# A weight ring of four slots instead of five, a 49th resident weight chunk, and two TensorE steps moved by a chunk

## The chip, the cores and the metric

The kernel runs on one core of one Trainium2 chip. The time is device microseconds from start to end of one execution; the figure for a kernel is the median over its runs. One execution was also taken by the hardware profiler; it has its own time, and a span from its first to its last instruction.

## The reference, cut to what matters

Two independent parts are computed and put side by side in the output. Part A is a shift and a long convolution over 2048 positions and 1024 channels. Part B is an attention over 64 segments of 32 tokens with 8 memory tokens that are handed from segment to segment:

```python
for s in range(n_seg):
    h = concatenate([mem, x[:, s*32:(s+1)*32]])          # 40 tokens x 1024
    q, k, v = (einsum('btd,dhe->bhte', h, W) for W in (Wq, Wk, Wv))   # 32 heads of 128
    p = softmax(where(mask, q @ k.T * scale, -1e9))
    o = einsum('bhte,hed->btd', p @ v, Wo)
    mem = o[:, :8]                                        # needed by the next segment
    outs.append(o[:, 8:])
```

Segment s + 1 can't begin before segment s has its memory rows, so part B is a chain of 64 segments. Each of them multiplies by all of Wq, Wk, Wv and Wo, 32 MB in bf16, while the on-chip memory (SBUF) holds less than that.

## The kernel before, in words

**Chunks.** The weights of part B are cut into 64 chunks of 128 x 2048 bf16 (512 KB): `(m, kc, g)` for K (m = 0), Q (1) and V (2), with eight slices kc of the contracted dimension and two halves g of the heads; `(3, hp, 0)` for Wo, two heads each. `ORDER` (L25 to L27) lists them in the order in which a segment uses them, and a chunk is called here by its place in that list, 0 to 63: K half 0 and Q half 0 interleaved (0 to 15), K half 1 (16 to 23), Q half 1 (24 to 31), V half 0 (32 to 39), V half 1 (40 to 47), Wo (48 to 63).

**Resident and streamed.** `STREAM` (L28) names the chunks that don't stay in SBUF: 16, of which two (56 and 57, `KEPT_A` and `KEPT_B`) are copied into spare room in PSUM and one small tile during segment 0. The other 14 are loaded anew in each segment from a copy in DRAM, `WS`. The other 48 chunks are resident, in tiles that the trace calls Wmid, Wres, Wmore, Wlate, pw and Wring.

**The ring.** Streamed chunks go through the slots of a ring: tiles `wring0`, `wring1`, `wring3` to `wring5`, in the order of the list `free` (L705). `fetch()` (L712) takes the next load of the list, takes the first free slot and issues the load on SP's queue (L716). `done(ch)` (L853) is called after a chunk's last matmul in the segment; it puts the slot back in the list and fetches. SP takes its instructions in the order written, so a load that waits for its slot holds back all behind it. Ahead of segment 0 two loads are issued (L745), and `RING - 2` more at the start of the loop (L886).

**Tiles with two lives.** `wring0` and `wring1` hold a transposed input (XBT) until the V matmuls ahead of the segments are through; `wring2` and `wring3` are the staging tiles (`pair`, L485) from which V of the new tokens is stored to DRAM (VBD<-pair). `wring2` then becomes the home of one resident chunk (L770), chunk 6, the first K chunk of the order's second group.

**Late loads.** `late` (L443, reordered in L747) lists resident chunks whose homes come free only near the end of part A; `place_late` (L722) takes the next of them and issues its load, also on SP. `at_hand` names V chunks that still lie in another chunk's home during segment 0; there `done` issues that home's load.

**A segment** (L1033 to L1107) is written out by hand inside `tc.manual_schedule()`, so instructions go to each engine in the order of the text; ahead of it a planner sets the order. `Proj.run(n)` (L922) issues n chunks of a projection, four matmuls of 128 x 512 each, and calls `done` after each chunk. `evac` (L934) lets ScalarE cast the result to bf16 (L936). `transposes` (L939, matmuls in L942) turns it on TensorE into the tile `tps`, from which it is copied to KT or QT. `scores` (L945), `softmax_a` (VectorE, then an exponential on ScalarE, L962), `softmax_b` (VectorE), `attend` (L988) and `evac_o` (a ScalarE cast of the attended values to OT, L1004) follow for each half. The output product (`out_half`, L1014) uses a Wo chunk in two passes f, each of four matmuls of 128 x 256; the four chunks of FIRST and the five of LAST do all their f = 0 passes before the first f = 1 pass, so a streamed chunk among them is held longer. POOL issues the loads of a segment's input (rec, L869) and of its part of V (VBs, L907) and the stores of the output (L1106).

Of the kernel before, what the change touches and what calls it, by code (L numbers as in the profile page):

```python
# [9 lines left out]
BF = mybir.dt.bfloat16  # L10
# [14 lines left out]
ORDER = [(0, kc, 0) for kc in (0, 1, 4, 5)] + [(1, kc, 0) for kc in (0, 1)] + [(0, kc, 0) for kc in (2, 3, 6, 7)] + \  # L25
    [(1, kc, 0) for kc in range(2, 8)] + [(m, kc, 1) for m in (0, 1) for kc in range(8)] + \
    [(2, kc, g) for g in range(2) for kc in range(8)] + [(3, hp, 0) for hp in O_ORDER]  # L27
STREAM = (1, 7, 13, 18, 24, 30, 35, 41, 46, 49, 53, 56, 57, 58, 60, 62)  # L28
N2, N3 = 12, 19
WO_COPY = 29  # L30
Q_LOAD = (10, 13, 16, 19)
X_LOAD = 1
RING = 5

PITCH = 2048
SCRATCH = 1024
# [383 lines left out]
def b_kernel(ctx: ExitStack, tc, x, mem0, Wq, Wk, Wv, Wo, outb, n_seg, run_a):  # L420
# [13 lines left out]
    streamed = set()  # L434
    for i in STREAM:
        streamed.add(order[i])
# [6 lines left out]
    late = [ch for ch in resident if ch not in placed]  # L443
# [12 lines left out]
    def stream_src(ch):  # L456
        return WS[ring_order.index(ch), :, 0:2048]
# [18 lines left out]
    base = ctx.enter_context(tc.tile_pool(name="b0_base", bufs=1, side="right", reuse_waits="tile"))  # L476
# [3 lines left out]
    def xbt(kc):  # L480
        return XBT[kc // 4][:, kc % 4]
# [3 lines left out]
    def pair():  # L485
        turns["pair"] ^= 1
        return base.tile([128, 2048], BF, tag=f"wring{2 + turns['pair']}", name="pair")

    def slot16(shape, dt, name):
        turns["stage"] ^= 1  # L490
        return base.tile(shape, dt, tag=f"stage{turns['stage']}", name=name)
# [3 lines left out]
    def pw(k=None):  # L495
        if k is None:
            k = pw_next[0] % 8
            pw_next[0] += 1
        return pring.tile([128, 2048], BF, tag=f"pw{k}", name="pw")
# [63 lines left out]
    def group(m, g, temps={}, which=range(8), ws=None, eng=nc.sync, held=False):  # L563
        ws = ws or [None] * 8
        for kc in which:
            ch = (m, kc, g)
            if ch in res:
                got.append(eng.dma_start(res[ch], dram_chunk(ch)))
                ws[kc] = res[ch]
            else:  # L570
                t = temps[ch]() if ch in temps else pw()
                got.append(eng.dma_start(t[:], dram_chunk(ch)))
                if ch in streamed:
                    copies.append((stream_src(ch), t[:]))
                ws[kc] = t[:]
        while copies and not held:
            copied.append(nc.gpsimd.dma_start(*copies.pop(0)))
        return ws
# [28 lines left out]
    def evac(dst, src):  # L607
        flip[0] += 1
        if flip[0] % 3:
            nc.scalar.copy(dst, src)  # L610
        else:
            nc.vector.tensor_copy(dst, src)
# [35 lines left out]
    def store():  # L648
        if stores:
            nc.scalar.dma_start(*stores.pop(0))  # L650
# [40 lines left out]
    def more(i):  # L691
        return wres3.tile([128, 2048], BF, tag=f"Wmore{i}", name="Wmore")
# [5 lines left out]
    order_s = [ch for ch in order if ch in streamed]  # L698
    kept = {KEPT_A: "A", KEPT_B: "B"}
    at_hand = {}  # L700
# [1 line left out]
             if s == 0 and ch not in v_temp[2:] or s > 0 and ch not in kept]  # L702
    live = {}
    now = [0]
    free = [4, 5, 0, 1, 3]  # L705

    def slot():
        k = free.pop(0)
        t = (base if k < 4 else ring).tile([128, 2048], BF, tag=f"wring{k}", name="wring")
        return k, t  # L710

    def fetch():  # L712
        if loads:
            s, ch = loads.pop(0)
            live[s, ch] = k, t = slot()
            nc.sync.dma_start(t[:], stream_src(ch))  # L716

    def place(ch, ap):
        res[ch] = ap
        nc.sync.dma_start(dst_view(ap, ch), dram_chunk(ch))  # L720

    def place_late(n, tile_of):  # L722
        chs = [late.pop(0) for _ in range(n)]
        t = tile_of()
        for i, ch in enumerate(chs):
            place(ch, t[:, 2048 * i:2048 * i + 2048])
# [4 lines left out]
    with c0p:  # L731
        temps = dict(zip(v_temp, homes_v))
        wv = [group(2, 0, temps), None]
        for _ in rest:
            store()
        wv[1] = group(2, 1, temps)
        for i, ch in enumerate(v_temp):
            if i >= 2:
                home = (lambda i=i: more(i)) if i < len(v_temp) - 2 else (lambda k=i - len(v_temp) + 4: pw(k))
                at_hand[ch] = (wv[ch[2]][ch[1]], home)  # L740
        while stores:
            store()
        with tc.issue_after(got[-1].ins):
            for _ in range(2):
                fetch()  # L745
        n_k = len(own[0, 0])
        late = late[n_k:-1] + late[4:n_k] + late[:4] + late[-1:]  # L747
        for g in range(2):
            ws = wv[g]
            if g == 0:  # L750
                vsts = slot16([128, 4, 4, 512], BF, "vst")
            for tb in range(4):
                vst = vsts[:, tb] if g == 0 else pair()[:].rearrange("p (c w) -> p c w", c=4)
                for c in range(4):
                    ps = ps0.tile([128, 512], F32, tag="ps0", name="vb_ps")
                    for kc in range(8):
                        nc.tensor.matmul(ps[:], lhsT=xbt(kc)[:, 16 * tb:16 * tb + 16, :].rearrange("p s t -> p (s t)"),  # L757
                                         rhs=ws[kc][:, c * 512:(c + 1) * 512], start=(kc == 0), stop=(kc == 7))
                    evac(vst[:, c, :], ps[:])
                nc.scalar.dma_start(  # L760
                    VBD[16 * tb:16 * tb + 16, :, :, :, g * 128:(g + 1) * 128].rearrange("s t c i e -> (s t) (c i) e"),
                    vst.rearrange("p c (i e) -> p (c i) e", i=4))
            if g == 0:
                with tc.issue_after(got[-1].ins):
                    place_late(4, stage_home)
                    for i in [*range(len(v_temp) - 2, n_more), *range(len(v_temp) - 2)]:
                        place_late(1, lambda: more(i))
                    place_late(1, lambda: pw(2))
                    place_late(4, stage_home)
        place_late(1, lambda: base.tile([128, 2048], BF, tag="wring2", name="Wring"))  # L770
        assert len(late) == len(at_hand)

    one = ctx.enter_context(tc.tile_pool(name="b_one", bufs=1, side="right", reuse_waits="tile"))
    two = ctx.enter_context(tc.tile_pool(name="b_two", bufs=2, side="right", reuse_waits="tile"))
# [39 lines left out]
    def keep(ch):  # L814
        t = live[0, ch][1]
        if kept[ch] == "A":
            w = t[:].bitcast(I32).rearrange("p (hh dh f x) -> p hh f dh x", hh=2, dh=2, f=2)
            for q in range(4):
                bits(OTi[:, q, 160:416].rearrange("p (dh x) -> p dh x", dh=2), w[:, q // 2, q % 2])
        else:  # L820
            w = t[:].bitcast(I32)
            for q in range(4):
                for home, at in B_homes[q]:
                    n = home.shape[1] * (home.shape[2] if len(home.shape) == 3 else 1)
                    if len(home.shape) == 3 and n > 128:
                        for dh, o in enumerate(quarter_cols(q)):
                            bits(home[:, 2 * dh:2 * dh + 2, :], w[:, o // 2:o // 2 + 128].rearrange("p (b x) -> p b x", b=2))
                        continue
                    for dh, o in enumerate(quarter_cols(q)):
                        lo, hi = max(at, 128 * dh), min(at + n, 128 * dh + 128)  # L830
                        if lo < hi:
                            src = w[:, o // 2 + lo - 128 * dh:o // 2 + hi - 128 * dh]
                            bits(home if len(home.shape) == 3 else home[:, lo - at:hi - at], like(src, home))
# [19 lines left out]
    def done(ch):  # L853
        if now[0] == 0 and ch in at_hand:
            place_late(1, at_hand[ch][1])
        elif ch in streamed and (now[0] == 0 or ch not in kept):
            if now[0] == 0 and ch in kept:
                keep(ch)
            free.append(live.pop((now[0], ch))[0])
            fetch()  # L860

    P_pad = one.tile([128, 5, 64], BF, name="P_pad")
# [22 lines left out]
    with tc.manual_schedule():  # L885
        for _ in range(RING - 2):  # L886
            fetch()
# [14 lines left out]
        for s in range(n_seg):  # L902
# [133 lines left out]
            q0 = Proj(1, 0)  # L1036
            fill_mem(hT, Y, 1)
            q0.run(2)
            k0 = k0.run(4).evac()
            q0.run(3)  # L1040
            KT0 = keys(0)
            nc.vector.tensor_copy(KT0[:, :, :, 0:32], transposes(k0))  # L1042
            q0 = q0.run(3).evac()
            k1 = Proj(0, 1).run(4)
            QT0 = one.tile([128, 4, 4, 32], BF, tag="QT", name="QT")
            nc.vector.tensor_copy(QT0[:], transposes(q0))
# [11 lines left out]
            V0 = pv0.run(4).evac()  # L1058
            scores(1, QT1, KT1)
            E1 = softmax_a()  # L1060
            pv1 = Proj(2, 1).run(4)
            attend(0, PT0, V0)
            OT0 = evac_o(0)
            PT1 = softmax_b(E1)
            pv1.run(4)
            if not last:
                load_x(s + 1)
            V1 = pv1.evac()
# [110 lines left out]
```

## Time and profile before

| what | us |
|---|---|
| median of 3 runs | 1865.01 (1863.74 to 1870.66) |
| the profiled execution's own time | 1864.63 |
| its span | 1862.8 |
| TensorE busy | 1737.2 |
| VectorE busy | 1009.7 |
| ScalarE busy | 680.8 |
| POOL busy | 267.2 |
| start of segment 1's VBs load, and of segment 63's | 486.0, 1839.0 |
| mean rate of the DMA engines | 340 GB/s |

"Busy" counts the time in which an engine executes, not the time in which its sequencer waits or issues. The page cuts the span in 40 slices of 46.6 us and gives the busy share of each in tenths. In a time line, a row has start and duration in us, engine, line of the kernel, operation, tiles (out<-in) and shapes; the bracket at its end is the idle time of the engine before the row and what ended it. PE is TensorE's matmuls, PEld its weight loads. A queue of DMA issues has a q behind its engine's name (SPq). Matmuls overlap, so their durations add to more than the time they take: the steps between their starts tell more.

### The profile page before, as it was taken

How to read it: one execution, taken by the hardware profiler on the slowest of the kernel's cores; microseconds unless marked ns; L12 is line 12 of the kernel's file. 1: busy time of each engine (PE TensorE's matmuls, PEld its weight loads, DVE VectorE, ACT ScalarE, POOL GpSimd, SP SyncE). 2: the span in 40 equal slices, each digit the busy share in tenths (PEclk: the TensorE clock that was granted, in tenths of full speed). 3: DMA queues.
4: the chain of work that ended last, by engine and by line, in shares of the span. 5: the costliest groups of instructions: out<-in, count | busy, mean ns of one | idle time of the engine just before them, and what ended most of it. 6: DMA issues, size and time to landing. Idle time of an engine off the chain costs nothing.

```text
span 1862.8 us, 68333 instructions
## 1 busy us (share of the span) xinstructions
PE 1737.2 (93%) x29492; PEld 1000.3 (54%) x29492; DVE 1009.7 (54%) x3391; ACT 680.8 (37%) x1195; POOL 267.2 (14%) x501
## 2 busy tenths in 40 slices
PE   6989996767999999999999999999999999999998
PEld 3433322323565666666566655566566656566665
DVE  9927873201555555555555555555555555555555
ACT  6945650111333333333333333333333333333333
POOL 4003341000111111111111111111111111111111
PEclk9999998888999999999999999999999999999999
DMA  9989889996999999999999999999999999999997
GB/s 333 372 301 316 291 270 326 309 307 197 343 353 358 357 352 359 352 352 356 360 357 356 349 338 351 352 368 356 350 355 357 353 349 354 351 363 358 348 360 292
DMA packets 232946, 632.45 MB, mean 340 GB/s; under 512 B 72818, under 2 KB 72834, under 8 KB 232644
## 3 DMA queue, kind: packets, MB, share of 16 engines
q1 hardware_dynamic: 160548, 558.83, 81.4%
q0 software_dynamic: 17344, 46.17, 6.8%
q10 hardware_dynamic: 54752, 23.07, 4.6%
q8 instruction: 231, 3.78, 0.8%
q14 instruction: 71, 0.58, 0.1%
HBM read 572.94 MB, written 58.72 MB: 339 GB/s over the span
## 4 chain that ended last, share of the span: by engine, by line
PE 68%; DMA 20%; ACT 5%; DVE 5%; issue 2%; ACTq 0%; POOL 0%; POOLq 0%; DVEq 0%; SPq 0%
PE acc L927 26%; PE yacc L1014 20%; DMA wring<-WS 15%; PE kb_ps L621 6%; PE tps L942 4%; PE vb_ps L757 3%; DMA REC<-stage 2%; ACT OT L1004 2%; ACT qkv_sb L936 1%; ACT s_sb L246 1%; DVE mx L957 1%; DVE E L959 1%; PE tps L874 1%; PE OTp L992 1%; PE s_ps L244 1%
## 5 line engine op out<-in xcount | busy, mean ns | idle before, releaser
L1014 PEld LDWEIGHTS <-OT 128*64 128x64 bf16 x8255 | 438.7, 109 | 63.2 <-ACT OT L1004 36.6
L927 PEld LDWEIGHTS <-rec 128*32 128x32 bf16 x12288 | 282.7, 96 | 294.8 <-DVE rec L881 34.8
L936 ACT CAST qkv_sb<-acc 128x512 bf16<-128x512 f32 x384 | 224.8, 585 | 388.0 <-PE acc L927 384.1
L927 PE MATMUL acc<-Wres,rec 128*32 128x512 bf16 x3328 | 248.8, 380 | 0.3 <-issue 0.3
L1014 PE MATMUL yacc<-Wmore,OT 128*64 128x256 bf16 (+1 forms) x3072 | 244.7, 273 | 0.0
L1014 PE MATMUL yacc<-wring,OT 128*64 128x256 bf16 (+1 forms) x2576 | 231.5, 275 | 8.0 <-DMA wring<-WS 6.9
L927 PE MATMUL acc<-wring,rec 128*32 128x512 bf16 x2300 | 225.8, 381 | 6.8 <-DMA wring<-WS 6.0
L927 PE MATMUL acc<-Wmid,rec 128*32 128x512 bf16 x3072 | 222.6, 381 | 0.0
L1104 ACT CAST Y<-yacc 128x256 bf16<-128x256 f32 x128 | 47.6, 372 | 275.8 <-DVE quarter_b L790 181.2
L790 DVE TENSOR_SCALAR quarter<-OTp 128x256 int32<-128x256 int32 x252 | 99.8, 417 | 80.6 <-ACT OT L1004 80.6
L927 PE MATMUL acc<-pw,rec 128*32 128x512 bf16 x1796 | 142.4, 381 | 0.0
L1004 ACT CAST OT<-OTp 128x640 bf16<-128x640 f32 x128 | 87.5, 684 | 144.8 <-PE OTp L996 144.8
L1106 POOL DMA_DIRECT2D out_dram<-Y x128 | 63.7, 502 | 507.1 <-ACT Y L1104 507.1
L927 PE MATMUL acc<-Wlate,rec 128*32 128x512 bf16 x1536 | 128.2, 381 | 1.0 <-issue 0.8
L881 DVE COPY rec<-tps 128x32 bf16<-128x32 bf16 x128 | 22.4, 175 | 191.3 <-PE tps L874 189.7
L942 PEld LDWEIGHTS <-qkv_sb 128*128 128x128 bf16 x1024 | 57.9, 98 | 112.8 <-ACT qkv_sb L936 107.7
L1042 DVE COPY KT<-tps 128x512 bf16<-128x512 bf16 x64 | 27.2, 425 | 158.8 <-PE tps L942 158.8
L942 PE MATMUL tps<-ident,qkv_sb 128*128 128x128 bf16 x1024 | 101.8, 222 | 6.2 <-ACT qkv_sb L936 0.7
L957 DVE TENSOR_REDUCE mx<-SB 128x8 f32<-128x320 f32 x128 | 62.9, 492 | 82.3 <-PE SB L951 82.2
L1014 PE MATMUL yacc<-Wlate,OT 128*64 128x256 bf16 x1024 | 101.0, 276 | 5.7 <-ACT OT L1004 0.2
L869 POOL DMA_DIRECT2D rec<-REC x64 | 36.3, 566 | 452.3 <-PE acc L927 444.8
L962 ACT ACTIVATE E<-E 128x320 f32<-128x320 f32 x128 | 60.1, 469 | 76.4 <-DVE E L959 76.4
(220 smaller groups left out, 2512.1 us busy)
## 6 DMA issues: line engine op xcount, KB each, us to landing
wring<-WS SPq DMA_DIRECT2D x897, 512.0 KB, 6.0
rec<-REC POOLq DMA_DIRECT2D x64, 192.0 KB, 5.3
SK<-s_sb SPq DMA_DIRECT2D x16, 512.0 KB, 5.1
SU<-s_sb SPq DMA_DIRECT2D x16, 512.0 KB, 5.0
Kg<-SK SPq DMA_DIRECT2D x32, 256.0 KB, 4.7
Ug<-SU SPq DMA_DIRECT2D x32, 256.0 KB, 5.4
REC<-stage ACTq DMA_DIRECT2D x16, 512.0 KB, 10.8
zt<-SZ SPq DMA_DIRECT2D x16, 512.0 KB, 7.8
```

The lines of the kernel that those rows point to most:

```text
L621: nc.tensor.matmul(ps[:], lhsT=ws[kc][:, hl * 128:(hl + 1) * 128], rhs=xbt(kc).rearrange("p s t -> p (s t)"), start=(kc == 0), stop=(kc == 7))
L757: nc.tensor.matmul(ps[:], lhsT=xbt(kc)[:, 16 * tb:16 * tb + 16, :].rearrange("p s t -> p (s t)"), rhs=ws[kc][:, c * 512:(c + 1) * 512], st ...
L790: nc.vector.tensor_scalar(out=dst, in0=src, scalar1=0, scalar2=None, op0=ALU.bitwise_or)
L927: nc.tensor.matmul(self.acc[32 * c:32 * c + 32, :], lhsT=hT[:, ch[1], :], rhs=w[:, 512 * c:512 * c + 512], start=(ch == chs[0]), stop=(ch ...
L936: nc.scalar.copy(sb[:], self.acc[:])
L942: nc.tensor.transpose(tp[:, i * 128:(i + 1) * 128], sb[:, i * 128:(i + 1) * 128], ident[:])
L957: nc.vector.tensor_reduce(out=mx[:], in_=S, op=ALU.max, axis=AX.X)
L962: nc.scalar.activation(E[:], E[:], ACT.Exp, scale=scale)
L1004: nc.scalar.copy(OT[:], o_view)
L1014: nc.tensor.matmul(yacc[f][64 * dh:64 * dh + m, x - o:y - o], lhsT=lhsT, rhs=r, start=(h == 0 and x == o), stop=stop, tile_position=(0, 64 ...
L1104: nc.scalar.copy(Y[:, 256 * f:256 * f + 256], yacc[f][:, 0:256])
L1106: nc.gpsimd.dma_start(bass.AP(outb.tensor, outb.offset + SEG * s * 2048 + 512 * dh, [[2048, 32], [1, 512]]), Y[64 * dh + NM:64 * dh + 40, :])
```

## The change

The ring has four slots (0, 1, 4, 5), and the streamed chunks are 15 instead of 16, most of them at other places of the order: 13 loads a segment instead of 14. Both `wring2` and `wring3` become homes of resident chunks, 49 in all; their loads are issued in segment 0 when the second streamed chunk (7) is done, ahead of that point's fetch, and they are the ones of Wo chunks that are used late. Chunk 6 and the others of `late` move up to homes that come free earlier. In each segment the transposes of K half 0 stand behind four chunks of Q instead of three, with two instead of three behind them, and the first attention stands behind three chunks of V half 1 instead of four, with five instead of four behind it.

```diff
-STREAM = (1, 7, 13, 18, 24, 30, 35, 41, 46, 49, 53, 56, 57, 58, 60, 62)
+STREAM = (1, 7, 13, 20, 24, 30, 36, 42, 47, 52, 54, 56, 57, 58, 62)
...
-RING = 5
+RING = 4
...
-    free = [4, 5, 0, 1, 3]
+    free = [4, 5, 0, 1]
...
-        late = late[n_k:-1] + late[4:n_k] + late[:4] + late[-1:]
+        late = late[n_k:-3] + late[4:n_k] + late[:4] + late[-3:]
...
-        place_late(1, lambda: base.tile([128, 2048], BF, tag="wring2", name="Wring"))
-        assert len(late) == len(at_hand)
+        assert len(late) == len(at_hand) + 2
...
             free.append(live.pop((now[0], ch))[0])
+            if now[0] == 0 and ch == order_s[1]:
+                for k in (2, 3):
+                    place_late(1, lambda: base.tile([128, 2048], BF, tag=f"wring{k}", name="Wring"))
             fetch()
...
             k0 = k0.run(4).evac()
-            q0.run(3)
+            q0.run(4)
             KT0 = keys(0)
             nc.vector.tensor_copy(KT0[:, :, :, 0:32], transposes(k0))
-            q0 = q0.run(3).evac()
+            q0 = q0.run(2).evac()
...
-            pv1 = Proj(2, 1).run(4)
+            pv1 = Proj(2, 1).run(3)
             attend(0, PT0, V0)
             OT0 = evac_o(0)
             PT1 = softmax_b(E1)
-            pv1.run(4)
+            pv1.run(5)
```

## The prediction

> **What bounds the kernel now.** I read the page first, then the windows of the segment loop, then its time lines.
>
> ```profile
> PE   6989996767999999999999999999999999999998
> ...
> DMA  9989889996999999999999999999999999999997
> ...
> wring<-WS SPq DMA_DIRECT2D x897, 512.0 KB, 6.0
> ```
>
> From slice 11 on (the 64 segments) TensorE and the DMA engines both stand at 9, and one transfer makes nearly all the traffic: the ring's loads. The window over segments 1 to 62 says how full each is:
>
> ```profile
> 486.00:1839.00 1353.00, 1326.52 (x26854) 824.03 (x26850) 740.23 (x2790) 467.81 (x868) 166.71 (x373) 1.00 0.96 354
> ```
>
> TensorE's clock is whole (1.00), the DMA share is 0.96 at 354 GB/s. The 62 segments take 1353.0/62 = 21.82 us each. The POOL time line marks them by the VBs load:
>
> ```profile
> 1096.93 0.53 POOL L907 DMA_DIRECT2D VBs<-VBD  x1 [0.17 <-issue]
> ...
> 1119.77 0.54 POOL L907 DMA_DIRECT2D VBs<-VBD  x1 [0.17 <-issue]
> ...
> 1228.73 0.54 POOL L907 DMA_DIRECT2D VBs<-VBD  x1 [0.17 <-issue]
> ...
> 1250.05 0.53 POOL L907 DMA_DIRECT2D VBs<-VBD  x1 [0.17 <-issue]
> ```
>
> The best takes 1250.05 - 1228.73 = 21.32 us, another 1119.77 - 1096.93 = 22.84. The work is the same, so 21.32 is TensorE's floor with every weight at hand, and 21.82 - 21.32 = 0.50 us a segment (31 us in all) is waiting for the ring. Each landing's time, from SP's instructions in two stretches of one segment:
>
> ```profile
> DMA to landing us min/median/max: 6.5/6.8/7.1
> ...
> DMA to landing us min/median/max: 4.4/5.2/6.0
> ```
>
> The first is 1229.0 to 1233.5, where loads are issued close together, the second 1244 to 1250, where they are further apart. So a landing holds a queue of 1 to 2 us in the first third of a segment.
>
> **Step 1: one load fewer, one slot fewer.** A segment moves 354 GB/s x 21.82 us = 7.72 MB. Without one 524,288-byte load it is 7.20 MB, or 20.3 us at the rate now reached: under the floor, so the DMA engines stop being the bound and the queue should go. Against it stands the slot. Each of the four slots serves 13/4 loads a segment, so a load has 21.3 x 4/13 = 6.6 us for issue, landing, waiting and use (now 21.82 x 5/14 = 7.8). I laid out TensorE's order with the durations of the trace (0.216 us a chunk of a projection, 0.218 a half chunk of the output, 0.105 at each switch between them and transposes) and took, for every load, the time from the release of its slot to its first use. With the new STREAM these budgets are 5.83, 5.94, 5.49, 5.67, 5.96, 6.25, 6.69, 5.76, 6.20, 6.72, 6.32, 6.60 and 6.21 us for chunks 1, 7, 13, 20, 24, 30, 36, 42, 47, 52, 54, 58, 62 (now 5.64 to 8.72). Of a budget 0.15 us goes to issue and pick-up.
>
> The trace has no four-slot ring, so the landing is bounded from two sides. Lightest rows: over the last 60 segments, the landings of chunks 13 and 18 have medians 4.95 and 4.86 us (95% under 6.11 and 5.67); with the other four light ones (1, 7, 60, 62) the median is 5.2. Heaviest: chunk 35, 7.27, whose budget of 7.48 is the one that is most often missed now (0.15 us a segment before it). Drawing landings at random from the rows of 13 and 18 and laying them on the new budgets gives 0.21 us of stalls a segment, from the six light rows 0.40. The same sum for the ring of now, with each chunk's own rows, gives 0.37 where 0.50 was measured, so it is somewhat low; on the other side, the light rows still hold some of the backlog that a full queue leaves on the slowest engine. In the new order, issues stand 1.0 to 2.5 us apart, 1.62 on average, which is the spacing of today's light rows (1.5 to 2.0). I take **0.24 us**; below is 0, above the rivals' figures.
>
> Rule against row: the Trainium skill's HBM Reference, Specifications (TRN2), says that a core streaming alone reaches about 425 GB/s. By that, 7.72 MB would need 18.2 us, DMA would not bind and a load removed would bring nothing; the trace's 354 at a share of 0.96 says otherwise, and I go by the trace. Its SBUF page (SBUF — State Buffer, The DMA setup-cost knee) gives about 2 us plus bytes over 436 GB/s, an estimate of 3.2 us for a ring load, by which no budget would ever be missed; the rows show 4.9 to 7.3.
>
> **Step 2: the K transposes one chunk later.**
>
> ```profile
> 1229.10 0.82 PE L927 MATMUL acc<-Wmid,rec 128*32 128x512 bf16 x12
> ...
> 1229.37 0.58 ACT L936 CAST qkv_sb<-acc 128x512 bf16<-128x512 f32 x1 [2.10 <-PE acc L927]
> 1230.01 0.23 PEld L942 LDWEIGHTS <-qkv_sb 128*128 128x128 bf16 x4 [0.58 <-ACT qkv_sb L936]
> ```
>
> Three Q chunks start at 1229.10 and would be through at 1229.10 + 3 x 0.216 + 0.105 = 1229.85; the transposes start at 1230.01, held by ScalarE's cast, which ends at 1229.95. So 0.16 us is lost in each segment. A fourth chunk fills it: 1230.07, 0.06 after the cast. The Q cast and its transposes keep four chunks between them; QT, scores and all behind move up alike. Gain 0.16 x 63 = 10 us, if no ring wait takes it. New floor 21.32 - 0.16 = **21.16 us**.
>
> **Step 3: the first attention one chunk earlier.** Behind it on ScalarE stands evac_o (L1004), and the output product waits for that:
>
> ```profile
> 1237.96 0.58 ACT L936 CAST qkv_sb<-acc 128x512 bf16<-128x512 f32 x1 [0.46 <-PE acc L927]
> 1239.14 0.47 ACT L962 ACTIVATE E<-E 128x320 f32<-128x320 f32 x1 [0.60 <-DVE E L959]
> 1239.52 0.67 ACT L1004 CAST OT<-OTp 128x640 bf16<-128x640 f32 x1
> ```
>
> The attention's last matmuls start at 1238.93, but OT starts only behind the second softmax's exponential, which hangs on scores(1), not on the attention. So the move brings nothing. It adds a wait for V's cast (ends 1238.54; the attention would come at 1238.82 - 0.22 = 1238.60): 0 to 0.05 us, with five V chunks queued behind it on TensorE, and it is taken from the 0.18 us that the output product waits for OT anyway (it could start at 1240.07 and starts at 1240.25). Cost 0, or 3 us in all without that cover.
>
> **Step 4: segment 0.**
>
> ```profile
> 446.76 9.43 DMA VBD<-pair
> ...
> 456.28 3.09 DMA Wring<-in_B_Wk_dram
> ...
> 459.41 0.62 PE L927 MATMUL acc<-Wring,rec 128*32 128x512 bf16 x4 [11.03 <-DMA Wring<-in_B_Wk_dram]
> ```
>
> Chunk 6, kept in wring2, can be loaded only when the last V store has left that tile (456.2): TensorE stands 11.0 us. In the change this chunk has a home in a stage tile, loaded at 424 to 430, so the wait goes. But the two loads into wring2 and wring3 are now issued by SP when chunk 7 is done, near 448.7, and SP stands at wring2 until the same 456.2, with the load of chunk 30 and all later ones behind it. Then come three loads at once: the first lands like Wring after 3.1 us, at 459.4, the others 1.3 to 1.4 apart, so chunk 30 at about 462.2. TensorE is there at 454.9 and waits some 7 us. Now it starts that chunk at 467.99, so 5.8 us are gained. Against this, the matmuls after the wait of now run at half pace (0.43 us a chunk at 459.8 to 461.1, about 1.3 us lost in all); the new wait costs the same, later. Net **4.5 us**, with bounds 2 (the output's loads, already late by 2.3 us at 480 to 482, wait more with four slots) and 9 (chunk 30 comes with the first of the loads).
>
> Before the segments one WS copy falls away and the resident loads get other homes, beside 53 us of V matmuls on TensorE: 0.
>
> **Sum.** A segment 21.16 + 0.24 = 21.40 us; (21.82 - 21.40) x 62 = 26.0, segment 0 4.5, the last segment's K wait 0.16: 30.7 us. The profiled execution took 1864.63 us (span 1862.8), 0.4 under the median of 1865.01. 1864.6 - 30.7 = **1834 us**.
>
> **Rivals.**
> A, all ring stalls vanish: a segment at 21.16 gives 0.66 x 62 = 41, with 4.5 to 9 in segment 0: 1815 to 1819. For it: 20.3 us of traffic under a floor of 21.16. Against: landings vary by 1 us, and budgets are down to 5.5.
> B, the landing stays at today's median, 6.0: laid on the budgets, chunks 1, 13 and 42 come late, the segment becomes 22.0, +11 against -4.7 from segment 0: about 1871; at 5.75 the segment is 21.57 and the total 1844. With B the shorter ring eats what the missing load gives.
> C, slower: the ring's depth becomes the bound. It decides from a landing of about 6.0 us on; at 6.5, today's level in the crowded third, the segment is 23.5 and the total 1860 + 102 = 1962. Place: SP's issues for chunks 13 and 42. For it: medians of 6.0 to 7.3 in eight of fourteen rows now. Against: those rows are behind a queue that a saturated engine makes.
> D, the load removed is hidden anyway and only steps 2 and 4 tell: 1864.6 - 10 - 4.5 = 1850.
>
> **How the numbers follow.** The forecast 0.58 (own range 1822 to 1846), A 0.12, D 0.10, B 0.10, C 0.10. Range 1815 to 1862: it takes in A, D and the nearer half of B. About 0.5% (9 us) is what a measurement of this kernel can tell from no change. Faster by that: forecast, A, D and a little of B, 0.82; within it 0.09; slower 0.09.
>
> **What would show it.** VBs issues about 21.4 us apart; DMA share in the segments near 0.92 and the rate near 338 GB/s; landings of 4.5 to 5.7 us; the K transposes' weight load no longer ended by the cast; OT still right behind the exponential; in segment 0 no wait at chunk 6, and one of 7 us at chunk 30, ended by a wring load. Wrong it would be made by landings that stay at 6 us or above, by waits before chunks 13, 20 and 42 in most segments, or by a granted clock below 1.00.

## The result and the profile after

The changed kernel takes 1871.47 us (median of 11 runs, 1863.64 to 1881.68), the kernel before in the same session 1866.41 (11 runs, 1863.58 to 1870.66): a ratio of 1.0035, interval 1.002 to 1.005. Forecast were 1834 us and a range up to 1862, so direction and size were wrong: one load of fourteen less, and the kernel is no faster. Of all executions below one, of five slots with 14 loads at other places, ran at a granted clock of 0.65 and took 2437.91 us; it is left out of that kernel's figures.

The profiled execution took 1879.17 us (span 1877.4). That is 7.7 us above the median, and its segments show the stalls somewhat larger than the typical run does.

The page of the changed kernel, as it answers to that of before:

```profile
PE   6989995768999999999999999999999999999998
...
DMA  9989889897899999999999989899999999999887
...
wring<-WS SPq DMA_DIRECT2D x833, 512.0 KB, 5.5
```

The DMA row, all 9 in the segments before, now has slices at 8, and a landing has a median of 5.5 us instead of 6.0. The window over segments 1 to 62 (length, then busy us of the engines, TensorE's clock, DMA share, GB/s) of the changed kernel:

```profile
483.82:1853.43 1369.61, 1327.02 (x26846) 825.98 (x26842) 741.41 (x2790) 469.44 (x868) 166.77 (x373) 1.00 0.92 326
```

The clock stayed at 1.00, and the DMA share is the 0.92 that was forecast. But that share was forecast for shorter segments: the 62 segments take 1369.61/62 = 22.09 us each, where 21.40 was forecast and 21.82 stood before. The DMA engines are busy 0.92 x 22.09 = 20.3 us in a segment, where it was 0.96 x 21.82 = 20.9; in a segment of 21.16 us the 20.3 would again be a share of 0.96. The 0.92 comes of the waiting, and doesn't show that the engines have room. TensorE's busy time is the same (1327 us in both), so all of the difference is waiting. The VBs issues of its best segment, and of a slow one (8 of the 62 take that long), in POOL's time line:

```profile
683.87 0.54 POOL L909 DMA_DIRECT2D VBs<-VBD  x1 [0.16 <-issue]
...
705.03 0.53 POOL L909 DMA_DIRECT2D VBs<-VBD  x1 [0.17 <-issue]
...
1232.58 0.54 POOL L909 DMA_DIRECT2D VBs<-VBD  x1 [0.17 <-issue]
...
1255.54 0.53 POOL L909 DMA_DIRECT2D VBs<-VBD  x1 [0.17 <-issue]
```

The best segment takes 705.03 - 683.87 = 21.16 us, the forecast floor to the hundredth, which is luck in part: three of the runs below, with the same TensorE order, have a best of 21.08. The other takes 22.96. By the best segments the floor fell by 0.16 us, and the waiting above it rose from 0.50 to 22.09 - 21.16 = 0.93 us a segment. The groups of the page name what is waited for (busy us, mean ns | idle before them, what ended most of it); first the kernel before:

```profile
L1014 PE MATMUL yacc<-wring,OT 128*64 128x256 bf16 (+1 forms) x2576 | 231.5, 275 | 8.0 <-DMA wring<-WS 6.9
...
L927 PE MATMUL acc<-wring,rec 128*32 128x512 bf16 x2300 | 225.8, 381 | 6.8 <-DMA wring<-WS 6.0
```

and the changed one:

```profile
L929 PE MATMUL acc<-wring,rec 128*32 128x512 bf16 x2300 | 226.4, 383 | 27.3 <-DMA wring<-WS 26.1
...
L1016 PE MATMUL yacc<-wring,OT 128*64 128x256 bf16 x2064 | 169.8, 275 | 17.7 <-DMA wring<-WS 17.0
```

12.9 us of TensorE's idle time were ended by a ring load before, 43.1 us after (8 us of these in segment 0). The rows leave out idle times under 0.15 us. Taken by the steps between the matmuls' starts instead, against the run with half the bytes below, 0.94 of the 0.99 us by which a segment of the change exceeds that run's median stand at matmuls of streamed chunks. The chain of waits of the changed kernel through the slow segment shows the form of one such wait (start, us, what):

```profile
1243.30 1.22 PE acc L929 x20
1244.52 0.02 issue
1244.54 6.58 DMA wring<-WS
1251.12 0.04 issue
1251.16 1.72 PE yacc L1016 x28
```

TensorE ends the last use of chunk 47 at 1244.52; that frees a slot, SP issues the load of chunk 62 at once, and it lands 6.58 us later. TensorE, four streamed chunks further on, stands there. No engine and no queue is late in this chain: it is one turn of a slot, release to release, and the next turn begins where this one ends.

Where the 45 us between forecast and profiled span (1832.1 and 1877.4) went: segments 1 to 62, 1369.6 instead of 1327.0, 42.6; up to segment 1, 483.8 instead of 486.0 - 4.5 = 481.5, 2.3; the rest behind the last VBs issue.

### The profile page after: what moved, and what is told of

Read it like the earlier page. It is cut to its first block, busy times and chain, and to the rows that moved or that the text cites. A ratio compares the mean times of both kernels' runs of the same rounds, so it can differ in the third digit from the quotient of the medians.

```text
span 1877.4 us, 68207 instructions
## 1 busy us (share of the span) xinstructions
PE 1741.2 (93%) x29492; PEld 1004.6 (54%) x29492; DVE 1011.2 (54%) x3391; ACT 682.6 (36%) x1195; POOL 266.6 (14%) x500
## 4 chain that ended last, share of the span: by engine, by line
PE 60%; DMA 29%; DVE 5%; ACT 3%; issue 2%; POOL 0%; ACTq 0%; SPq 0%; POOLq 0%; DVEq 0%
PE acc L929 25%; DMA wring<-WS 24%; PE yacc L1016 17%; PE kb_ps L621 5%; PE tps L944 3%; PE vb_ps L757 2%; DMA REC<-stage 2%; ACT s_sb L246 1%; ACT OT L1006 1%; PE tps L876 1%; DMA VBD<-pair 1%; PE s_ps L244 1%; DVE E L961 1%; DVE mx L959 1%; PE OTp L994 1%
## 5 line engine op out<-in xcount | busy, mean ns | idle before, releaser
L929 PE MATMUL acc<-Wres,rec 128*32 128x512 bf16 x3328 | 226.0, 381 | 0.0
L929 PE MATMUL acc<-Wmid,rec 128*32 128x512 bf16 x3072 | 210.3, 379 | 0.0
L1016 PE MATMUL yacc<-Wmore,OT 128*64 128x256 bf16 (+1 forms) x2560 | 207.6, 274 | 0.0
L1016 PE MATMUL yacc<-wring,OT 128*64 128x256 bf16 x2064 | 169.8, 275 | 17.7 <-DMA wring<-WS 17.0
L1016 PE MATMUL yacc<-Wring,OT 128*64 128x256 bf16 (+1 forms) x1024 | 93.4, 274 | 0.0
```

The costliest lines, as they stand in the source:

```text
L929: nc.tensor.matmul(self.acc[32 * c:32 * c + 32, :], lhsT=hT[:, ch[1], :], rhs=w[:, 512 * c:512 * c + 512], start=(ch == chs[0]), stop=(ch ...
L1016: nc.tensor.matmul(yacc[f][64 * dh:64 * dh + m, x - o:y - o], lhsT=lhsT, rhs=r, start=(h == 0 and x == o), stop=stop, tile_position=(0, 64 ...
```

## The experiments

The theory: four slots leave a load 5.5 to 6.7 us from issue to use, and the landings of 512 KB are about that long, now above and now below; every miss stalls TensorE. Rivals: the traffic still binds; the other three steps cost the time; the places in the order are wrong; the hand-over of the slots itself is slow; one colliding transfer makes the landings late. The 2 x 2 of load count and depth comes first.

**The change with five slots, 13 loads.**

```diff
-RING = 4
+RING = 5
...
-    free = [4, 5, 0, 1]
+    free = [4, 5, 0, 1, 3]
...
-                for k in (2, 3):
-                    place_late(1, lambda: base.tile([128, 2048], BF, tag=f"wring{k}", name="Wring"))
+                place_late(1, lambda: base.tile([128, 2048], BF, tag="wring2", name="Wring"))
+                res[late.pop(0)] = list(res.values())[-1]
```

> The changed kernel with its fifth ring slot kept (wring3), 13 loads a segment as in the change. The 49th resident chunk has no home then, so Wo chunk 61 is multiplied with the data of chunk 60: part of the output is not the reference's, the work is the same. Depth theory (four slots leave a load less time than its landing takes): ring waits go, segments of 21.2 to 21.3 us instead of about 22.0, total 1871 - 0.7 x 62 = about 1826 us. Traffic theory (the DMA engines are still the bound with 13 loads): no change, 1866 to 1875. Order theory (the moved TensorE steps brought waits of their own): no change, 1866 to 1875.

Measured: 1813.16 us, ratio 0.9735 (0.9719 to 0.9752). A segment takes 21.22 us on average, 21.08 at best. Its window over the segments, and its source view of the ring's load (who waited for it: us, times; last line, landing):

```profile
482.00:1795.00 1313.00, 1304.67 (x26819) 816.97 (x26818) 739.98 (x2789) 466.19 (x867) 166.73 (x372) 1.00 0.96 340
...
  PE acc L929: 5.5, 4
  PE yacc L1016: 1.4, 1
...
DMA to landing us min/median/max: 4.2/5.6/8.9
```

The landings are as long as in the change (5.6 and 5.5); only the time to use is longer. The same loads with one slot more hardly stall: 1.1 of these 6.9 us stand in segments 1 to 62. And the DMA engines are as full as in the kernel before, 0.96, with a load less. So a share of 0.96 is no bound by itself, and 13 loads leave the engines no emptier once TensorE keeps its pace.

**The kernel before with four slots, 14 loads.**

```diff
-RING = 5
+RING = 4
...
-    free = [4, 5, 0, 1, 3]
+    free = [4, 5, 0, 1]
```

> The kernel before with one slot taken away and nothing else: 14 loads a segment through slots 0, 1, 4, 5, wring3 unused. Depth theory: waits at chunks 13, 18 and 62 in nearly every segment, segments of 23 to 24 us, total 1940 to 2000 us. Traffic theory: a slot more or less does not matter, 1866 to 1880 us.

Measured: 2014.82 us, ratio 1.0808 (1.0783 to 1.0834), 24.26 us a segment. The same view of this kernel:

```profile
  PE yacc L1014: 83.5, 97
  PE acc L927: 51.9, 78
...
DMA to landing us min/median/max: 3.2/5.3/10.6
```

A slot less costs the kernel before 150 us, though its landings get shorter (5.3 against 6.0), with fewer loads under way. So the time a slot takes to come round counts as much as the landing.

**The change with half the bytes in each load**, everything else the same:

```diff
-            nc.sync.dma_start(t[:], stream_src(ch))
+            n = 2048 if s == 0 else 1024
+            nc.sync.dma_start(t[:, 0:n], stream_src(ch)[:, 0:n])
```

(The matmuls take columns 1024 to 2047 of such a chunk from its first half again.)

> The changed kernel, four slots, 13 loads a segment at the same places and the same releases, but from segment 1 on each load brings only the first 1024 of the chunk's 2048 columns, which the matmuls use twice (half of each streamed chunk is left out, so part of the computation changes; the matmuls' number and shapes don't). Theory (what costs the time is the landing against the budget of 5.7 to 6.7 us that four slots leave): with half the bytes a landing should come well under 5 us, the waits for the ring go, a segment takes 21.1 to 21.2 us as in the five-slot run, 1812 to 1822 us in all. Rival 1 (the hand-over of the slots itself, SP's issue and the order of the places, costs the time, whatever the transfer's size): segments stay near 22.0, 1865 to 1873 us. Rival 2 (a landing is mostly a fixed cost, so half the bytes shorten it by under 0.5 us): 1840 to 1860 us.

Measured: 1817.60 us, ratio 0.9742 (0.9716 to 0.9768), 21.18 us a segment. The page of this kernel:

```profile
L933 PE MATMUL acc<-wring,rec 128*32 128x512 bf16 x2300 | 225.4, 382 | 5.8 <-DMA wring<-WS 5.8
...
L1020 PE MATMUL yacc<-wring,OT 128*64 128x256 bf16 x2064 | 168.7, 275 | 3.4 <-DMA wring<-WS 3.4
...
wring<-WS SPq DMA_DIRECT2D x819, 256.0 KB, 3.1
```

With four slots, the same places and the same hand-over, a landing of 3.1 us lets every wait for the ring in segments 1 to 62 go (what the rows still show stands in segment 0). That excludes slots, places and SP as the cause by themselves. The table holds the cases together (mean over 62 segments of the profiled runs, with the DMA share in them; the time to turn a slot round is floor x slots / loads):

| kernel | slots, loads | turn of a slot | landing, median | DMA share | mean segment | ratio to before |
|---|---|---|---|---|---|---|
| before | 5, 14 | 7.6 | 6.0 | 0.96 | 21.82 | 1 |
| change | 4, 13 | 6.5 | 5.5 | 0.92 | 22.09 | 1.0035 |
| five slots | 5, 13 | 8.1 | 5.6 | 0.96 | 21.22 | 0.9735 |
| before, four slots | 4, 14 | 6.1 | 5.3 | 0.91 | 24.26 | 1.0808 |
| half the bytes | 4, 13 | 6.5 | 3.1 | 0.58 | 21.18 | 0.9742 |

**The K transposes' move alone**, in the kernel before:

```diff
-            q0.run(3)
+            q0.run(4)
...
-            q0 = q0.run(3).evac()
+            q0 = q0.run(2).evac()
```

> The kernel before with the transposes of K half 0 behind four chunks of Q instead of three, and nothing else. If the step's 0.16 us a segment reach the end: 1866 - 10 = 1856 us. Ring theory (a segment that starts its next chunk earlier meets the next ring load earlier, and waits there): most of it is eaten, 1860 to 1866 us. Order theory (the move costs): above 1866.

Measured: 1861.52 us, ratio 0.9988 (0.9977 to 0.9999). The best segment falls by 0.18 us to 21.14, the mean by 0.03: what TensorE gains it waits for at the ring. The idle time before ring matmuls that a load ended grows from 12.9 to 20.1 us.

**The change without the K and the attention move.**

```diff
-            q0.run(4)
+            q0.run(3)
...
-            q0 = q0.run(2).evac()
+            q0 = q0.run(3).evac()
...
-            pv1 = Proj(2, 1).run(3)
+            pv1 = Proj(2, 1).run(4)
...
-            pv1.run(5)
+            pv1.run(4)
```

> The changed kernel with the two moved TensorE steps put back (K transposes behind three Q chunks, attention behind four V chunks); ring, places and late loads as in the change. Ring theory: the floor rises by 0.16 us but the ring sets the time, 1868 to 1875 us, within 4 of the change. If the steps were worth their 10 us in the change: about 1881. Order theory (they cost): 1855 to 1866.

Measured: 1882.57 us, ratio 1.0105 (1.0083 to 1.0128), 11 us above the change. My ring theory's 1868 to 1875 missed: I had thought that the ring would swallow the steps here as well. The floor without the moves is 21.35, with them 21.17, and the 0.18 us a segment are kept, 62 x 0.18 = 11 us. (In the two profiled executions the mean segments differ by 0.11 us only, 22.20 and 22.09.) Why the step is kept here, and in the kernel before not, stays open. That full DMA engines set the mean there is one reading, but the run with five slots stands at the same share of 0.96 without such waits.

**Segment 0 alone**, in the kernel before, with `wring2` alone as late home:

```diff
-        late = late[n_k:-1] + late[4:n_k] + late[:4] + late[-1:]
+        late = late[n_k:-2] + late[4:n_k] + late[:4] + late[-2:]
...
-        place_late(1, lambda: base.tile([128, 2048], BF, tag="wring2", name="Wring"))
-        assert len(late) == len(at_hand)
+        assert len(late) == len(at_hand) + 1
...
             free.append(live.pop((now[0], ch))[0])
+            if now[0] == 0 and ch == order_s[1]:
+                place_late(1, lambda: base.tile([128, 2048], BF, tag="wring2", name="Wring"))
```

> The kernel before (five slots, 14 loads, its places, its TensorE order) with step 4 alone: chunk 6 and the others of late get the earlier homes, and wring2 takes a Wo chunk whose load is issued when chunk 7 is done in segment 0. Segment 0 is 4 to 5 us shorter and the other segments stay: 1866 - 4 = 1859 to 1863 us. Rival (what segment 0 gains, the later loads of that segment give back): within 2 us of the kernel before.

Measured: 1857.65 us beside 1864.47 of before, ratio 0.9966 (0.9951 to 0.9982): 6.8 us, somewhat more than the 4 to 5 that were expected.

**Four slots, other places**, laid out so that the tightest budgets grow:

```diff
-STREAM = (1, 7, 13, 20, 24, 30, 36, 42, 47, 52, 54, 56, 57, 58, 62)
+STREAM = (0, 7, 13, 19, 24, 30, 36, 41, 46, 51, 53, 56, 57, 58, 61)
```

> The changed kernel with the 13 streamed chunks at other places: 0, 7, 13, 19, 24, 30, 36, 41, 46, 51, 53, 58, 61. They were chosen with a small model of the ring whose landings are fitted to the runs so far; it gives the change's own places 21.95 us a segment and these 21.69. Depth theory (what counts is the time from a slot's release to the next use of it, against landings of 5 to 6 us): 1871 - 0.26 x 62 = about 1855 us, with less waiting at chunks 24 and 62. If the places do not matter beside the number of slots: 1868 to 1875.

Measured: 1869.82 us, ratio 1.0031 (1.0019 to 1.0043): no different from the change, so the model's 1855 missed. The wait before the last streamed chunk shrinks from 0.27 to 0.15 us a segment and that before 24 from 0.21 to 0.13; those before 58 (0.12) and 30 (0.09) stay. Part of that is the spread between executions: that of the run with the input's load later, with the change's own places, has 0.18 and 0.17 in place of 0.27 and 0.21. The mean segment is 21.88 us, 0.80 above this kernel's best. The turns of the slots add up to slots times period wherever the places are, and none of the two orders gets free of the misses.

**The attention's place undone**, in the change:

```diff
-            pv1 = Proj(2, 1).run(3)
+            pv1 = Proj(2, 1).run(4)
...
-            pv1.run(5)
+            pv1.run(4)
```

> The changed kernel with the first attention back behind four V chunks, the K step kept. The run with both steps undone was some 11 to 13 us slower than the change, which is what the K step alone should be worth. If so, this one is within 2 us of the change (1869 to 1873). If the attention's place matters for the ring (the release of chunk 42's slot, the time from 42 to 47), 1874 to 1880 us.

Measured: 1869.52 us, ratio 1.0037 (1.0019 to 1.0055), beside 1.0035 of the change. The move is worth nothing.

**The input's load later**, in the change:

```diff
-            if not last:
-                load_x(s + 1)
             V1 = pv1.evac()
...
             out_proj((4,), OT0)
+            if not last:
+                load_x(s + 1)
```

> The changed kernel, with the load of the next segment's input (rec, 192 KB) issued about 2.2 us later, behind the first five output chunks. In the changed kernel it is issued at the same moment as the ring's load of chunk 62, before which TensorE waits the most (0.27 us a segment). If the two loads share the DMA engines to chunk 62's loss, its landing falls from 5.6 to 5.1 to 5.3 us, its wait to about 0.1, and the total by 8 to 11 us, to 1860 to 1863. If the wait only moves on to chunks 58, 1 or 24, as it did when the places were changed, or the landing is late for its own four predecessors, then 1867 to 1873. If the input itself then comes late for the next segment, over 1875.

Measured: 1867.16 us (1861.1 to 1876.42), ratio 1.0002 (0.9975 to 1.0028). Chunk 62's landing hardly moves, 5.51 us for 5.56, and in 59% of the segments TensorE starts on it within 0.05 us of the landing, as it does after a wait; in the change it was 65%. So the collision is not why it is late. Whether the load's place is worth the 4 us between the medians is open: the two intervals overlap.

**Five slots and 14 loads at other places, with the K and the segment 0 step.** The two diffs above on the kernel before, and

```diff
-STREAM = (1, 7, 13, 18, 24, 30, 35, 41, 46, 49, 53, 56, 57, 58, 60, 62)
+STREAM = (3, 9, 14, 19, 24, 29, 35, 40, 44, 49, 52, 55, 56, 57, 59, 63)
```

> The kernel before (five slots, 14 loads) with three edits: K transposes behind four Q chunks, step 4 of the change for wring2, and the streamed chunks at 3, 9, 14, 19, 24, 29, 35, 40, 44, 49, 52, 55, 59, 63. The same model gives 21.49 us a segment against 21.72 with the old places. Depth theory: 1862 (the K step alone, as run) - 0.23 x 62 - 4 = about 1844 us. If the 14th load keeps the DMA engines the bound whatever the places: 1857 to 1862 us.

Measured: 1845.75 us, ratio 0.9913 (0.9889 to 0.9936), 21.53 us a segment at a DMA share of 0.98 (359 GB/s). So 14 loads can go faster than in the kernel before, whose 0.96 wasn't the engines' limit. And with the input's load later as well:

> The version that was faster than both (five slots, 14 loads at other places, K transposes a chunk later, segment 0's second load moved), with the input's load 2.2 us later as well. There DMA is still nearly full, and a deeper ring rides over a late landing, so I expect little: 1843 to 1850, against 1849 without it. If the collision matters at a full queue too, 1838 to 1843.

Measured: 1845.86 us, ratio 0.9899 (0.9871 to 0.9926). The fifth slot stays, and what was right in the change is kept: this beats both kernels by about 1%. Against the line above it the input's place is again within the intervals.

## Why the prediction failed, step by step

**Step 1, the traffic: right that 13 loads don't bind, wrong that the queue would go.** With the slot kept the kernel is 58 us faster than the change, 0.14 us a segment above its best. But a load less didn't empty the DMA engines: busy 20.9 us a segment before, 20.3 in the change, 20.4 with five slots, a share of 0.96 at TensorE's pace as before. The forecast share of 0.92 was met by luck, in segments that were longer than forecast; with five slots and segments nearer the forecast it is 0.96.

**Step 1, the stalls: the term that failed.** "I take 0.24 us", with 0.40 from the six light rows; measured are 0.93 a segment, (0.93 - 0.24) x 62 = 43 us of the 45 by which the profiled execution is over the forecast. Two things were mis-sized.

The larger is the landing. I drew it from the rows of chunks 13 and 18 (4.95 and 4.86) because a queue of 1 to 2 us seemed to sit in the others and would go with the saturation. It went only in part: the median is 5.5 in the change and 5.6 with five slots, at shares of 0.92 and 0.96. That the landings stayed long because the engines stayed full is the likely reading; the run with half the bytes (3.1 us at 0.58) agrees, but changes size and share at once. From issue to the last of the load's semaphore events, over the last 60 segments, the change shows (budget: median time from issue to use in the run with half the bytes, where no load is waited for):

| chunk | budget forecast, less 0.15 | budget | landing, median | landing, 95% under | change's wait, us a segment |
|---|---|---|---|---|---|
| 24 | 5.81 | 5.74 | 5.78 | 6.91 | 0.21 |
| 30 | 6.10 | 6.03 | 6.12 | 7.02 | 0.10 |
| 58 | 6.45 | 5.67 | 5.15 | 6.17 | 0.10 |
| 62 | 6.06 | 5.51 | 5.56 | 6.93 | 0.27 |
| 13 | 5.34 | 6.04 | 5.78 | 6.67 | 0.03 |
| 20 | 5.52 | 5.46 | 4.58 | 5.57 | 0.02 |

Over all chunks the landing's median is 5.51 and 95% are under 6.68, so it lies across the budgets, and its spread costs more than its middle. I laid each chunk's own landings of the change on its budget in the sum of the prediction: drawn at random they give 1.1 us of stalls a segment (0.2 to 0.3 of it at each of 24, 30 and 62, where the trace has 0.21, 0.10 and 0.27), every one at its chunk's median only 0.17. So the rows of chunks 13 and 18 were not landings "without a queue" that other places would have too. When they were issued, 2.7 and 2.5 other ring loads were under way on average, the fewest in that kernel (up to 4.0); but in the change it is 2.1 to 3.0 at every chunk and the median is 5.5, so the number under way doesn't explain it, and why the two were short stays open.

The smaller is two budgets. Of the thirteen, ten are within 0.15 us of the budgets of that run. Chunk 58 was laid out 0.78 too long and 62 by 0.55, because I had put all eight quarter steps of the kept chunks ahead of chunk 58, while only two stand there; 13 was 0.70 too short. With the budgets mended, the sum gives 0.26 from rows 13 and 18 and 0.54 from the six light rows: not enough to save the forecast.

**Rivals.** C named the mechanism, the ring's depth as the bound, "from a landing of about 6.0 us on", and B's total of 1871 is the measured one, by luck. Both put the point too high and the place wrong: it began at a median of 5.5, since a spread of 2 us reaches the budgets before the median does, and the waits are before 24, 30, 58 and 62, hardly at 13 and 42. A, in which no stalls are left, is what five slots (1813) and half the bytes (1818) show.

**Step 2: right.** The best segment fell to 21.16. The matmul group of the transposes, before and then after (idle time in the third field):

```profile
L942 PE MATMUL tps<-ident,qkv_sb 128*128 128x128 bf16 x1024 | 101.8, 222 | 6.2 <-ACT qkv_sb L936 0.7
```

```profile
L944 PE MATMUL tps<-ident,qkv_sb 128*128 128x128 bf16 x1024 | 101.8, 222 | 0.3 <-ACT qkv_sb L938 0.3
```

The idle time ahead of them is gone. (The weight load's own row goes on naming the cast; it overlaps the matmuls.) "If no ring wait takes it" was the right proviso: alone in the kernel before the step gives 0.9988; in the change it stays.

**Step 3: right, nothing.** OT starts behind the exponential as before (ScalarE's time line of the changed kernel), and the run with the move undone agrees:

```profile
1243.34 0.47 ACT L964 ACTIVATE E<-E 128x320 f32<-128x320 f32 x1 [0.60 <-DVE E L961]
...
1243.72 0.67 ACT L1006 CAST OT<-OTp 128x640 bf16<-128x640 f32 x1
```

**Step 4: right, within its bounds.** From segment 0's VBs issue to segment 1's it is 47.3 us where it was 51.5: 4.2 instead of 4.5. One execution gives that to 2 us or so, since the run with half the bytes, whose segment 0 is the same, has 49.3. With the step alone it is 46.9. The chain of waits of the changed kernel goes as laid out, chunk 30's load behind the two into wring2 and wring3, and these behind the last V store:

```profile
447.82 8.54 DMA VBD<-pair
...
456.45 0.38 SPq L720
...
456.94 0.41 SPq L720
...
457.40 5.38 DMA wring<-WS
462.78 0.04 issue
462.82 2.75 PE acc L929 x24
```

TensorE goes on at 462.8 (forecast 462.2), after 5.7 us of idling (forecast some 7). The 2 us by which this kernel's segment 0 begins later are not part of it: with the same code ahead of the segments, the first VBs issue of the profiled runs lies between 429.9 (half the bytes) and 436.5 (change).

## What to carry to other kernels

A ring of loads has two limits: the bytes a turn moves, and the time one slot has to come round, which is the period times slots over loads. Set the second against the landings' upper end, not their median, and when a slot is given up for a resident tile, count what the other loads lose: here 13 loads on four slots (6.5 us a turn) were no better than 14 on five (7.6), while 13 on five (tried with one chunk's data doubled, for want of room) would have been 2.7% faster. Before counting on a shorter queue, work out the share that the DMA engines would have at the new pace: here it stayed at 0.96. And a light row of a crowded kernel is no price for a landing in another order; a run with the slot taken away, or with half the bytes, measures it directly.

## What the runs showed of the hardware

A 512 KB load landed in 5.5 us with the DMA engines at a share of 0.92, a 256 KB one in 3.1 us at 0.58, from the same places. The Trainium skill's SBUF page (SBUF — State Buffer, The DMA setup-cost knee) gives a fixed 2 us plus bytes over 436 GB/s, an estimate of 3.2 us and 2.6 us for the two sizes. The half load comes near it, the whole one doesn't: the second 256 KB cost 2.4 us here, 0.6 by the page. The page speaks of one transfer; here three or so were under way at a time (13 loads x 5.5 us in 22.1).
In the change 5% of the ring's landings take over 6.68 us and 5% under 4.46, for loads of one size. The DMA queue that the profile's page calls "instruction" may have a part in the spread:

```profile
q8 instruction: 231, 3.78, 0.8%
```

These are 231 packets of 16 KB, each about 1.05 us on one of the 16 DMA engines. Some 77% of the ring's loads meet one in their first 4 us. Compared chunk by chunk, these land 0.27 us later than the others in the change, 0.12 later in the kernel before. (Counted up to the landing itself the difference is larger, but a load that takes longer has more time to meet one.) A landing is counted here from the last of a load's 16 semaphore events, so one late event makes the load late. Whether these packets cause the spread was not tried.
